# Attention and a GELU layer on one core: eight weight pieces get buffers of their own and are loaded ahead of the second chunk's operands

## The chip, the core and the metric

One core of a Trainium2 chip. The metric is the device time of one execution in microseconds (us), less is better. The core has the engines TensorE (PE, with its weight loads shown as PEld), VectorE (DVE), ScalarE (ACT), GpSimd (POOL) and SyncE (SP); here SP only issues transfers from HBM, which run on 16 DMA engines shared by all queues.

## The reference

Masked attention with a distance bias over 4 batches, 8 heads, 768 positions, 64 values a head; its result, as 3072 rows of 512, goes through two products with a GELU between them.

```python
scores = scale * np.matmul(q, k.transpose(0, 1, 3, 2))
is_global = pos[None, :] < int(n_global)            # n_global = 8
is_local = (rel >= 0) & (rel < int(n_local))        # n_local = 96
...
scores = np.where(is_global | is_local, scores + bias, -1000000000.0)
a = softmax(scores)                                 # written out in the reference
x = (a @ v).transpose(0, 2, 1, 3).reshape(3072, 512)
h = x @ w_in                                        # w_in 512 x 2048, int64-backed words
g = 0.5 * h * (1.0 + erf(h * inv_sqrt2))
return g @ w_out                                    # w_out 2048 x 512
```

## The kernel before

The 3072 rows are done in 12 chunks of 256 rows, three to a batch. The hidden width of 2048 is cut into 8 slices of 256. A step `t` of the list `STEPS` is one chunk with one slice: `m1` makes `h` (24 matmuls for each half, L463), `gelu` turns it into `gh` and `gl` (L473, L474, L174), `m2` adds it to the chunk's sum `acc` (L493). The first two chunks run their slices in turns: (0,0), three empty steps, (1,0), (0,1), (1,1), (0,2) and so on. From the third chunk on, a chunk does its eight slices in a row, while the next chunk's attention is worked off between the steps.

The attention of a chunk c, head pair p, goes through `scores_pair` (PE, L340, tile `s`; then the masked reduction on DVE, L351), `exps` (ACT, L372; the scaling by 1/sum, L381, on DVE for the first two chunks, on POOL after that), `flip` (PE transposes, L391, tile `t`; copied by ACT to `pt`, L395) and `av_pair` (PE, L421). `split` scales the queries on POOL (L168). Chunk 0's operands are loaded by `load_first` into the pool `es`; those of a later chunk by `load` (`qr`, and `kr` in eight transfers for a middle chunk) and `load_v` (`vr`, six transfers), all on SP by L276. The buffers for `kr`, `qr` and `vr` of the later chunks exist once.

The weights arrive as 64-bit words, a slice in four pieces of 512 KB (pieces 0 and 1 are `win`, 2 and 3 `wout`). `load_words` (L176) issues a piece's load on SP (L179). `split_weights` makes a float of the words with one ACT instruction (L204) and three DVE instructions (L210, L212, L214); `part_weights` makes a high and a low half of it (ACT L224, DVE L174). The table `DECODE` says in which step each piece is split. A piece's ACT work is also ordered by hand behind the exponentials and GELUs of earlier steps, and its DVE work behind their reductions:

```python
ins = nc.scalar.activation(out=lw, in_=lw.bitcast(U32), func=AF.Copy, scale=2.0 ** -29).ins
if len(self.his) > 1:
    self.after(ins, self.his[-2], "a piece begins when ScalarE is through with the last but one")
if self.last_table is not None:
    self.after(ins, self.last_table, "a piece comes behind the exponentials of earlier steps")
```

All pieces of slices 0 to 6 go through the four buffers of the pool `ws`, in order. So piece n+4 can be loaded once piece n went through L214. Loads of weights keep their own order on SP, and those of chunk 2 stand behind the last piece of slice 2:

```python
if c == 2:
    self.after(ins.ins, self.word_ins[2, 3], "behind the first slices")
```

The order of instructions on each engine is otherwise made by the scheduler, which walks through the program with estimated times; an engine then works strictly in that order. `warm` matmuls (L359) with no use for the result stand between the first chunks' products, in counts fixed by hand. At the split of slice `LATE` the pool `es` is closed, and weights from that slice on are written where it was.

Of the kernel before, what the change touches and what calls it, by code (L numbers as in the profile page):

```python
# [31 lines left out]
NST = 8  # L32
# [16 lines left out]
DECODE.update({(1, i): i - 1 for i in range(4)})  # L49
DECODE.update({(s, i): 2 * s - 2 + i // 2 for s in range(2, NST) for i in range(4)})  # L50
FILL = {(0, 0, 0): 8, (0, 0, 1): 5, (0, 1, 1): 9, (0, 2, 1): 4, (0, 3, 1): 4, (1, 0, 1): 4}
LATE = 6
NEGMASK = -1000000000.0


# [8 lines left out]
def load_words2(nc, pool, src, name):  # L64
    w = pool.tile([P, 2, 2], I32, name=name + "_w")
    nc.scalar.dma_start(w.rearrange("p i t -> p (i t)"), src.bitcast(I32).partition_broadcast(P))
    return w
# [16 lines left out]
class Fast:  # L84
    def __init__(self, tc, ctx, qT, kT, v, w, out, limits):
        self.tc, self.nc = tc, tc.nc
        self.qT, self.kT, self.v, self.w, self.out = qT, kT, v, w, out
        self.limits = limits
        pool = lambda name, bufs=1, **k: ctx.enter_context(tc.tile_pool(name=name, bufs=bufs, **k))
        self.ctx = ctx  # L90
        self.early = ExitStack()
        self.es = self.early.enter_context(tc.tile_pool(name="es", bufs=1, side="right"))
        self.const = pool("const")
        self.wts = pool("wts")
        self.stg = pool("stg", 3)
        self.nat = pool("nat")
        self.pp = pool("pp", 6)
        self.ptp = pool("ptp", 2)
        self.xp = pool("xp", 3)
        self.gp = pool("gp", 2)  # L100
        self.sm = pool("sm", 2)
        self.words = ExitStack()
        self.ws = self.words.enter_context(tc.tile_pool(name="ws", bufs=4))
        self.ps_acc = pool("ps_acc", 2, space=PSUM)
        self.ps = pool("ps", 6, space=PSUM)
        self.win, self.wout = {}, {}
        self.kt, self.qt, self.vr, self.raw = {}, {}, {}, {}
        self.pt_n, self.pt_t, self.x = {}, {}, {}
        self.stat, self.g, self.h, self.acc = {}, {}, {}, {}
        self.last_table = self.last_word = self.last_dve = self.last_load = None  # L110
        self.his, self.word_ins, self.last_av, self.words_of = [], {}, None, {}
# [62 lines left out]
        return self.nc.vector.tensor_tensor(out=out, in0=in_, in1=hi.bitcast(F32), op=ALU.subtract)  # L174

    def load_words(self, s, i, use):  # L176
        pool, tag = (self.ws, "ws") if use == "w" and s < NST - 1 else (self.stg, "stage")
        w = pool.tile([P, 512, 2], I32, name=f"{use}{s}_{i}", tag=tag)
        ins = self.nc.sync.dma_start(w.rearrange("p f t -> p (f t)"), self.w[s * 4 + i]).ins  # L179
        if use == "w":  # L180
            if self.last_word is not None:
                self.after(ins, self.last_word, "weights in order")
            self.last_word = self.word_ins[s, i] = ins
        elif self.last_load is not None:
            self.after(ins, self.last_load, "behind the loads of earlier steps")
        return w
# [4 lines left out]
    def split_weights(self, s, i):  # L191
        nc = self.nc
        if i == 0:
            if s == LATE:
                self.early.close()
# [324 lines left out]
    def run(self, flag_i):  # L520
        wz = self.wz = self.es.tile([P, 512], F32R, name="wz")
        self.nc.vector.memset(wz.bitcast(F32), 0.0)
        self.warm_ps = self.ps_acc.tile([P, 512], F32, name="warm_ps", tag="ps_acc")
        self.warm(12)
        self.limit_words = load_words2(self.nc, self.const, self.limits, "nn")
        self.load_first()
        self.consts()
        for i in range(4):
            self.load_weights(0, i)
        self.load(1)  # L530
        self.load_v(1)
        for s in range(1, NST - 1):
            for i in range(4):
                self.load_weights(s, i)
        last = len(STEPS)
        for self.T in range(START[0] - 1, last):
            T = self.T
            first = 0 <= T + 1 < last and STEPS[T + 1] is not None
            second = T >= 0 and STEPS[T] is not None
            for (s, i), t in DECODE.items():  # L540
                if T == t + 1:
                    self.part_weights(s, i)
            for (s, i), t in DECODE.items():
                if T == t:
                    if s == NST - 1:
                        self.load_weights(s, i)
                    self.split_weights(s, i)
            if T == last - 8:
                self.flag(flag_i)
            k = T - 16 - GAP  # L550
            if 0 <= k < 64 and k % 2 == 0:
                self.check_load(k // 2)
            if 2 <= k < 66 and k % 2 == 0:
                self.check_words((k - 2) // 2)
            self.att(T, "load")
            self.att(T, "loadv")
            if first:
                self.m1(T + 1, 0)
            self.att(T, "pt", 0)
            if first:  # L560
                self.m1(T + 1, 1)
                self.gelu(T + 1)
            self.att(T, "pt", 1)
            self.att(T, "av")
            self.att(T, "s")
            if second:
                self.m2(T, 0)
            self.att(T, "exp")
            self.att(T, "split")
            if second:  # L570
                self.m2(T, 1)
# [200 lines left out]
```

## Time and profile before

| | us |
|---|---|
| median of 3 runs (698.00, 698.64, 701.43) | 698.64 |
| the profiled execution | 701.12 |
| its span from first to last instruction | 699.4 |
| PE busy in the span | 681.4 |

The profiled execution is a run of its own; 1.7 us of its time lie outside the span. PE is busy for 97% of the span, but its time per matmul is modelled with overlaps, so 97% busy doesn't mean 97% of what it could do. What the profile calls idle is time in which an engine waited for something.

### The profile page before, as it was taken

Reading aid. Unit: us, or ns where it says so; the run is one execution under the profiler, and the core shown is the slowest. Engines: PE = TensorE matmul, PEld = TensorE weight load, DVE = VectorE, ACT = ScalarE, POOL = GpSimd, SP = SyncE. Lnnn points to the kernel's source line nnn. Section 1 sums busy time; section 2 is a strip of 40 time slices with the busy share of each in tenths; the row PEclk is TensorE's granted clock in tenths of the full one; section 3 lists DMA queues with packets and bytes.
Section 4 is the critical chain, followed back from the end, with each engine's and each line's share of the span. In section 5 each row is a group of like instructions: output and inputs, shape, how many; then the busy total and the mean of one; then the engine's idle time right before and its main releaser. Section 6 shows DMA issues by size and latency. Waiting matters only on the chain.

```text
span 699.4 us, 14049 instructions
## 1 busy us (share of the span) xinstructions
PE 681.4 (97%) x5519; PEld 596.6 (85%) x5519; DVE 279.9 (40%) x969; ACT 356.4 (51%) x850; POOL 103.1 (15%) x232
## 2 busy tenths in 40 slices
PE   8989979999999999999999999999999999999996
PEld 6668867888899898898899899898988989988895
DVE  5988897522423423323323324224133243131210
ACT  3886787645435526626536446445356365362211
POOL 3102032201201201211021031031021031010000
PEclk9999999999999999999999999999999999999998
DMA  9728762331504314304144054033053152000000
GB/s 280 210 91 264 254 188 90 103 106 61 136 31 144 99 61 151 100 37 137 50 110 152 17 143 150 3 136 107 30 159 94 58 160 61 31 1 2 32 0 35
DMA packets 66041, 71.25 MB, mean 102 GB/s; under 512 B 32688, under 2 KB 49072, under 8 KB 65968
## 3 DMA queue, kind: packets, MB, share of 16 engines
q1 hardware_dynamic: 61520, 62.80, 29.8%
q10 hardware_dynamic: 4448, 7.48, 3.0%
q8 instruction: 46, 0.75, 0.4%
q14 instruction: 27, 0.22, 0.1%
HBM read 63.97 MB, written 6.29 MB: 100 GB/s over the span
## 4 chain that ended last, share of the span: by engine, by line
PE 89%; ACT 5%; DVE 3%; DMA 2%; issue 1%; POOL 0%; ACTq 0%; POOLq 0%
PE h L463 37%; PE acc L493 36%; PE av L421 6%; PE s L340 5%; PE t L391 4%; ACT n L372 2%; DMA w<-w 2%; PE warm_ps L359 1%; ACT L372 1%; ACT w L204 1%; DVE wb L212 1%; POOL n L381 0%; DVE wb L214 0%; DVE n L351 0%; ACT gh L473 0%
## 5 line engine op out<-in xcount | busy, mean ns | idle before, releaser
L463 PE MATMUL h<-xh,winh 128*128 128x256 f32 x768 | 221.5, 288 | 0.0
L463 PE MATMUL h<-xl,winh 128*128 128x256 f32 x768 | 217.9, 284 | 0.0
L463 PE MATMUL h<-xh,winl 128*128 128x256 f32 x768 | 217.8, 284 | 0.0
L174 DVE TENSOR_TENSOR gl<-gr,gh 128x512 fp32r<-128x512 f32 x96 | 69.0, 719 | 338.8 <-ACT gr L474 338.7
L493 PE MATMUL acc<-wouth,gh 128*128 128x512 f32 x384 | 157.0, 409 | 3.0 <-ACT gh L473 3.0
L463 PEld LDWEIGHTS h<-xh,winh 128*128 128x128 f32 x768 | 147.3, 192 | 5.4 <-issue 0.6
L493 PE MATMUL acc<-woutl,gh 128*128 128x512 f32 x384 | 150.6, 392 | 0.0
L463 PEld LDWEIGHTS h<-xl,winh 128*128 128x128 f32 x768 | 147.4, 192 | 3.7
L493 PE MATMUL acc<-wouth,gl 128*128 128x512 f32 x384 | 149.5, 394 | 0.0
L463 PEld LDWEIGHTS h<-xh,winl 128*128 128x128 f32 x768 | 147.2, 192 | 0.3 <-issue 0.2
L473 ACT ACTIVATE gh<-h 128x512 fp32r<-128x512 f32 x96 | 57.4, 598 | 173.0 <-PE h L463 170.1
L381 POOL TENSOR_SCALAR n<-n,su 128x192 f32<-128x192 f32 (+1 forms) x160 | 73.1, 475 | 457.0 <-ACT n L372 248.6
L395 ACT COPY pt<-t 128x384 f32<-128x384 f32 x96 | 45.6, 482 | 105.2 <-PE t L391 105.2
L493 PEld LDWEIGHTS acc<-wouth,gh 128*128 128x128 f32 x384 | 72.3, 188 | 22.4 <-issue 5.7
L493 PEld LDWEIGHTS acc<-wouth,gl 128*128 128x128 f32 x384 | 72.0, 188 | 16.9 <-issue 0.7
L493 PEld LDWEIGHTS acc<-woutl,gh 128*128 128x128 f32 x384 | 72.4, 189 | 12.5 <-issue 0.2
L372 ACT ACTIVATE n<-n,mn 128x192 f32<-128x192 f32 (+1 forms) x144 | 62.3, 434 | 1.5 <-DVE mn L351 1.3
L351 DVE CUSTOM_DVE_ANT_0 n<-s,pen 128x192 f32<-128x192 f32 (+1 forms) x192 | 55.2, 341 | 8.2 <-PE s L340 8.2
L474 ACT ACTIVATE gr<-h 128x512 f32<-128x512 f32 x96 | 56.9, 593 | 0.0
L391 PE MATMUL t<-ident,n 128*128 128x128 f32 x288 | 48.2, 275 | 4.5 <-POOL n L381 3.0
L421 PE MATMUL av<-pt,vr 64*64 64x64 f32 (+1 forms) x1024 | 46.7, 246 | 2.7 <-ACT pt L395 2.7
L421 PEld LDWEIGHTS av<-pt,vr 64*64 64x64 f32 (+1 forms) x1024 | 35.6, 135 | 13.9 <-issue 6.4
(74 smaller groups left out, 538.9 us busy)
## 6 DMA issues: line engine op xcount, KB each, us to landing
w<-w SPq DMA_DIRECT2D x32, 512.0 KB, 4.6
c<-w SPq DMA_DIRECT2D x32, 512.0 KB, 5.3
out<-o ACTq DMA_DIRECT2D x24, 256.0 KB, 2.0
qr<-qT SPq DMA_DIRECT2D x11, 512.0 KB, 4.0
vr<-v SPq DMA_DIRECT2D x22, 256.0 KB, 4.3
kr<-kT SPq DMA_DIRECT2D x16, 320.0 KB, 5.1
vr<-v SPq DMA_DIRECT2D x19, 192.0 KB, 2.8
kr<-kT SPq DMA_DIRECT2D x36, 64.0 KB, 4.1
```

What stands on the lines that cost most here:

```text
L174: return self.nc.vector.tensor_tensor(out=out, in0=in_, in1=hi.bitcast(F32), op=ALU.subtract)
L340: ins = nc.tensor.matmul(out, lhsT=lhs, rhs=rhs, start=True, stop=True).ins
L351: ins = nc.vector.tensor_tensor_reduce(out=nn[:, j * NK:j * NK + n], in0=sp[hh][:, j, 0:n], in1=pen, scale=-slope(2 * p + hh), scalar=3e38 ...
L372: self.table(nc.scalar.activation(out=nn, in_=nn, func=AF.Exp, bias=mn[:, i:i + 1], scale=-1.0, accum_out=su[:, i:i + 1]))
L381: ins = eng.tensor_scalar(out=nn, in0=nn, scalar1=su[:, i:i + 1], scalar2=0.0, op0=ALU.mult, op1=ALU.add)
L391: nc.tensor.transpose(tp[:, i, :], nn[:, o:o + P], self.ident)
L395: nc.scalar.copy(pt, tp)
L421: ins = nc.tensor.matmul(out, lhsT=lhs, rhs=rhs, start=start, stop=stop, skip_group_check=True).ins
L463: nc.tensor.matmul(hp[:, f, :], lhsT=w[:, d, f * P:(f + 1) * P], rhs=x[:, d, :], start=n == 0, stop=n == 3 * NP - 1)
L473: self.table(nc.scalar.activation(out=gh, in_=hp, func=AF.Gelu))
L474: self.table(nc.scalar.activation(out=gr, in_=hp, func=AF.Gelu))
L493: nc.tensor.matmul(acc, lhsT=g[:, f, ks], rhs=w[:, f, :], start=s == 0 and n == 0, stop=s == NST - 1 and n == 5)
```

## The change

Slices 0 and 1 get eight buffers of their own, one for each piece, in a new pool `rw` that is closed together with `es`. Their eight loads are issued directly behind those of the first chunk, ahead of `load(1)` and `load_v(1)`; before, only slice 0's four were. The four `ws` buffers serve slices 2 to 6 alone. `LATE` goes from 6 to 4, so that slices 4 to 6 are written into the room of `es` and `rw` and slices 0 to 3 stay in `wts`. No computation is added or taken away.

```diff
-LATE = 6
+LATE = 4
+SOON = 2
...
         self.es = self.early.enter_context(tc.tile_pool(name="es", bufs=1, side="right"))
+        self.rw = self.early.enter_context(tc.tile_pool(name="rw", bufs=1, side="right"))
...
-        pool, tag = (self.ws, "ws") if use == "w" and s < NST - 1 else (self.stg, "stage")
+        if use == "w" and s < SOON:
+            pool, tag = self.rw, f"rw{s}_{i}"
+        else:
+            pool, tag = (self.ws, "ws") if use == "w" and s < NST - 1 else (self.stg, "stage")
...
-        for i in range(4):
-            self.load_weights(0, i)
+        for s in range(SOON):
+            for i in range(4):
+                self.load_weights(s, i)
         self.load(1)
         self.load_v(1)
-        for s in range(1, NST - 1):
+        for s in range(SOON, NST - 1):
             for i in range(4):
                 self.load_weights(s, i)
```

## Rows read from the trace of the kernel before

**Rows 1.** The page: busy us of each engine with its share of the span and its number of instructions.

```profile
PE 681.4 (97%) x5519; PEld 596.6 (85%) x5519; DVE 279.9 (40%) x969; ACT 356.4 (51%) x850; POOL 103.1 (15%) x232
```

**Rows 2.** Busy time by stretches: from:to in us, length, then busy us (and instructions) of each engine, the granted TensorE clock as a share of full speed, the share of time that the DMA engines worked, and GB/s.

```profile
10.00:20.00 10.00, 9.27 (x73) 6.25 (x73) 6.83 (x37) 7.26 (x29) 1.85 (x4) 1.00 1.09 350
...
30.00:40.00 10.00, 10.00 (x94) 7.75 (x91) 9.78 (x37) 8.10 (x18) 0.00 (x0) 0.85 0.37 129
40.00:50.00 10.00, 7.90 (x85) 5.13 (x84) 7.64 (x29) 9.69 (x31) 0.00 (x0) 1.00 0.33 104
...
70.00:80.00 10.00, 10.00 (x74) 8.68 (x73) 9.57 (x18) 6.28 (x11) 0.00 (x0) 1.00 0.95 295
...
110.00:130.00 20.00, 19.15 (x167) 15.09 (x166) 15.71 (x38) 13.90 (x28) 4.18 (x4) 1.00 0.09 27
130.00:690.00 560.00, 559.96 (x4591) 500.89 (x4590) 172.08 (x663) 261.78 (x631) 78.64 (x184) 1.00 0.27 82
```

**Rows 3.** What PE waited for, in us in total, times, longest us: the first two rows from 0 to 60 us, the other two, which are all, from 60 to 130 us.

```profile
PE av L421 <- ACT pt L395: 2.7, 3, 1.3
PE t L391 <- DVE n L381: 1.5, 1, 1.5
...
PE acc L493 <- ACT gh L473: 3.0, 2, 2.3
PE t L391 <- POOL n L381: 3.0, 5, 1.5
```

**Rows 4.** The chain of work that ended last, between 78 and 90 us: start, length, what; and the matmul on PE at its end, from the timeline, with the idle time before it in brackets.

```profile
78.69 4.24 DMA w<-w
...
85.02 1.87 ACT n L372 x8
...
89.35 0.50 PE L493 MATMUL acc<-wouth,gh 128*128 128x512 f32 x1 [2.31 <-ACT gh L473]
```

**Rows 5.** What ACT and DVE waited for from 57 to 100 us: in total, times, longest.

```profile
ACT w L204 <- DMA w<-w: 6.7, 8, 1.4
...
DVE wb L210 <- DMA w<-w: 2.6, 2, 2.4
DVE su L374 <- ACT n L372: 1.3, 1, 1.3
```

**Rows 6.** The timeline of SP from 24 us: start, length, line, transfer, count.

```profile
24.83 28.39 SPq L179 DMA_DIRECT2D w<-w  x8
53.32 0.38 SPq L276 DMA_DIRECT2D qr<-qT  x1
...
68.45 52.85 SPq L179 DMA_DIRECT2D w<-w  x17
```

**Rows 7.** Timelines of DVE, ACT and PE: the first reduction of chunk 2's first and of its second head pair (the row before the second one on ACT is the GELU whose DVE work stands ahead of it), and the transpose on PE that waits for that pair.

```profile
81.93 0.34 DVE L351 CUSTOM_DVE_ANT_0 n<-s,pen 128x192 f32<-128x192 f32 x1
...
97.44 0.60 ACT L474 ACTIVATE gr<-h 128x512 f32<-128x512 f32 x1
...
99.56 0.35 DVE L351 CUSTOM_DVE_ANT_0 n<-s,pen 128x192 f32<-128x192 f32 x1
...
104.04 0.33 PE L391 MATMUL t<-ident,n 128*128 128x128 f32 x1 [1.49 <-POOL n L381]
```

**Rows 8.** The timeline of SP from 5 to 25 us: slice 0's words, then the second chunk's operands.

```profile
5.01 4.06 SPq L179 DMA_DIRECT2D w<-w  x4
9.11 0.43 SPq L276 DMA_DIRECT2D qr<-qT  x1
9.94 9.78 SPq L276 DMA_DIRECT2D kr<-kT  x8
19.77 4.95 SPq L276 DMA_DIRECT2D vr<-v  x6
```

**Rows 9.** Single transfers on SP's queue, size, us from issue to landing: slice 0's last piece (issued at 8.64 us), chunk 1's `qr` (at 9.11), its last `kr` (at 18.95) and its last `vr` (at 24.12).

```profile
w<-w SPq DMA_DIRECT2D x1, 512.0 KB, 7.6
qr<-qT SPq DMA_DIRECT2D x1, 512.0 KB, 8.4
...
kr<-kT SPq DMA_DIRECT2D x1, 64.0 KB, 4.2
...
vr<-v SPq DMA_DIRECT2D x1, 256.0 KB, 4.4
```

**Rows 10.** Timelines of PE, DVE and ACT: chunk 1's first scores, their first reduction, their first exponential, then chunk 0's last `av`, which waited for ACT, and chunk 1's first `av`.

```profile
23.94 0.88 PE L340 MATMUL s<-kr,qr 64*64 64x192 f32 x16
...
25.00 0.36 DVE L351 CUSTOM_DVE_ANT_0 n<-s,pen 128x192 f32<-128x192 f32 x1 [0.21 <-PE s L340]
...
26.19 0.47 ACT L372 ACTIVATE n<-n,nmax 128x192 f32<-128x192 f32 x1
...
29.30 0.53 PE L421 MATMUL av<-pt,vr 128*64 128x128 f32 x2 [1.33 <-ACT pt L395]
...
43.54 0.43 PE L421 MATMUL av<-pt,vr 128*64 128x128 f32 x2
```

**Rows 11.** All that ACT waited for from 24 to 50 us: in total, times, longest.

```profile
ACT n L372 <- DVE nmax L351: 1.3, 2, 1.0
ACT gh L473 <- PE h L463: 0.7, 1, 0.7
ACT wouth L224 <- DVE wb L214: 0.6, 1, 0.6
```

## Prediction

> **What bounds the kernel now.** I read the busy shares first: PE holds 681.4 of 699.4 us [rows 1]. Then the same by stretches [rows 2]: from 130 to 690 us PE is busy for 559.96 of 560 us at full clock. Nothing in the change touches that stretch, so every microsecond won or lost has to come from the first 130 us, and whatever is won there reaches the end undiminished. There PE does stop. The reader should see four kinds of waits [rows 3]: before 60 us for the copies of the attention (2.7 us) and for the scaled exponentials of chunk 1 (1.5); after 60 us for a GELU (3.0 us, of it one wait of 2.3) and for chunk 2's scaled exponentials (3.0). Third came the chain that ended last: ahead of the 2.31 us gap at 89.35 it runs back through ACT, through chunk 2's first exponentials, to a DMA of weight words that was under way from 78.69 to 82.93 [rows 4]. Fourth, the waits of ACT and DVE: in 57 to 100 us ACT stands 6.7 us, in eight places, and DVE 2.6 us in front of words that have not landed [rows 5]. So the words are late there, and they bound two engines that PE then waits for.
>
> Why they are late is in SP's timeline [rows 6]. Eight weight loads take from 24.83 to 53.2 us, since each must wait for a buffer; chunk 2's operands stand behind them by order and begin at 53.32; the next words stand behind those, up to 68.45. The DMA engines are only a third busy from 30 to 50 us and 95% busy from 70 to 80 [rows 2]: the transfers come in one heap.
>
> **Slice 1 leaves the ring of four.** No instruction is added; 32 loads of words remain 32. In 24 to 50 us, where slice 1 is split, ACT's waits name no DMA at all [rows 11]. So slice 1's own words were not late, and bringing them earlier is worth 0 in itself: their split is ordered behind the exponentials. The worth lies in what moves up behind them. Slice 2's four loads find their buffers free as soon as SP reaches them, at about 32 us (24.8 and the 5 to 6 us of the next part) where SP was still at them at 53 before. Chunk 2's operands, ordered behind them, need only chunk 1's buffers back, so the heap of 53 to 76 us is pulled apart into the quiet stretch. Slice 3's words are then no longer queued behind that heap; I take ACT's 6.7 us and DVE's 2.6 us of waits on words as gone.
>
> What that does for PE, gap by gap:
> - The 2.31 us at 89.35 [rows 4]. The floor of chunk 2's first exponentials is their reduction, which starts on DVE at 81.93 [rows 7], so they could begin at about 82.3 instead of 85.02 with the table already loaded. That is 2.7 us, more than the gap. It goes: 2.31.
> - The waits on POOL's scaling. The transpose at 104.04 follows the reduction at 99.56 by 4.48 us [rows 7]. DVE is full in front of it. Without the waits of rows 5 it would be 2.6 + 1.3 = 3.9 us further (the 1.3 is its wait for the exponentials just moved), that is 95.66. But the DVE work directly ahead needs the GELU that ends at 97.44 + 0.60 = 98.04; it moves up by the 2.31 only, to 95.73, and takes 0.6: the reduction starts at 96.33, the transpose can start at 100.81. PE gets there at 104.04 - 1.49 - 2.31 = 100.24. A wait of 0.57 is left. The waits around 104 sum to 2.1 (3.0 less the 0.85 idle of 110 to 130 us [rows 2, 3]), so 1.5 is won.
> - The 0.85 us of 110 to 130 us I leave as it is: DVE's lead is used up by then.
>
> Sum: 2.31 + 1.5 = 3.8 us won. Bounds: nothing, if the order on ACT and DVE puts other waits there; 2.31 + 2.1 + 0.85 = 5.3 if every gap goes. I take 3.8, since the DMA row is the direct cause of the larger gap.
>
> **Slice 1's words go ahead of chunk 1's operands.** Four pieces of 0.524 MB are now in front of 15 transfers on the same queue [rows 8]. From 10 to 20 us the DMA engines have no room, share 1.09 at 350 GB/s [rows 2]. Price of 2.10 MB: slice 0's last piece lands at 8.64 + 7.6 = 16.2 and the 512 KB behind it at 9.11 + 8.4 = 17.5 [rows 9], so 1.25 us a piece, 5.0 us for four; by the stretch's rate 2.10/350 = 6.0 us. Chunk 1's last `kr` landed at 18.95 + 4.2 = 23.15 and its first scores ran at 23.94 [rows 9, 10]; so there is 0.8 us to spare and not 5. The scores move to 28.2 to 29.2. `vr` lands at 28.5, then at 33.5 to 34.5, and its first reader is at 43.54 [rows 9, 10]: hidden.
>
> The Trainium skill, "DMA: Bandwidth & Descriptors", section "Queues, rings and completion order", says the same against the change: each DMA engine consumes a queue's descriptors in ring order, so operands can't overtake words. Its figure of some 358 GB/s per core from HBM would make it, as an estimate, 5.9 us; the measured 350 agrees, and the sum by it would be 0.4 us worse.
>
> What the lateness costs. The reduction of chunk 1's first pair starts 1.06 us after the scores and ACT could follow 0.36 us later; the exponentials at 26.19 become 29.6 to 30.6, later by 3.4 to 4.4. ACT had 1.0 + 0.7 + 0.6 = 2.3 us of idle time ahead of the first GELU [rows 11], and chunk 0's last `pt`, which now stood 1.33 us in PE's way [rows 10], can run in the hole instead. If the order fills the hole, 1.1 to 2.1 us are left; I take 1.6. Bounds: a gain of 1.3, if that PE gap goes and nothing replaces it; the whole 5.2 us, if PE stands in front of the scores with the rest behind it.
>
> **`LATE`, pools, addresses.** Slice 4 is written into the room of `es` and `rw`, whose last reader is the split of slice 1. That was done by 53.2 us, when the last load before chunk 2's took slice 1's last buffer; slice 4 is among the last 17 loads, from 68.45 on [rows 6]. The cover is 15 us, so this costs 0; without it ACT would wait for what is missing.
>
> **Sum.** 3.8 won, 1.6 lost: 2.2 us less. Against the profiled execution 701.12 - 2.2 = 698.9; that execution was 2.5 us above the median, and against the median it is 698.64 - 2.2 = 696.4 us. Half a percent, 3.5 us, is about what a measurement of this kernel can tell from no change, so the forecast is a small gain inside that. Chance 0.40; its own range, by 1.1 to 2.1 lost and 2.3 to 5.3 won, is 694.4 to 698.4.
>
> **Rivals.**
> 1. *The hole is filled entirely.* The scheduler knows of the later landing and runs chunk 0's tail first. For: PE idles 2.1 us from 40 to 50 and ACT waits for DVE and PE, so there is slack. Against: ACT is busy 9.69 of 10 us there [rows 2]. Then 0 is lost and 3.8 to 5.3 are won: 693.3 to 694.8, and 690.5 at best with the 1.3 us gap and the low-clock stretch (below) gone too. Chance 0.27.
> 2. *PE parks on chunk 1's scores (the slower side).* In place: 23.94 us. The scores keep their place in PE's order, and chunk 0's transposes, `av` and first `h` wait behind them. For: ACT's order already placed word work where it then waited eight times [rows 5], so the plan takes transfers to be earlier than they are. Price 4.2 to 5.2 us, and then the clock: after PE's gap of 1.33 us the granted clock fell to a mean of 0.85 in 30 to 40 us, the lower of its two levels, 1.2 GHz, for part of it [rows 2, 10], a loss of 1.5 us of work; a longer stop would add another such stretch. (The Trainium skill, "TensorE: Matmul & The Clock Gate", section "HAM oscillation", has the rule that waits for a DMA between groups of matmuls send the clock down; the row agrees.) With 3.8 won later that is 698.64 + 5.2 + 1.5 - 3.8 = 701.5; with only the first gap's 2.3 won it is 703.0. It decides from a stop of 3.8 us on. Chance 0.20, two thirds of it above 700 and about half above 702.1.
> 3. *The words are not the limit.* DVE is 9.57 of 10 us busy from 70 to 80, so earlier words only queue up in front of it, and the gaps move to another wait on DVE. Against: 2.6 us of DVE's own waits were for words. Then 0 is won: 698.64 + 1.6 = 700.2, or 698.6 if the head is hidden. Chance 0.13.
>
> **How the numbers follow.** Time 696.4, the likeliest case. Faster by over 0.5% (below 695.1): rival 1 and a quarter of the forecast's own spread (0.40 x 0.2 = 0.08), 0.35. Slower (above 702.1): half of rival 2 and the worst of rival 3, where both fall together, with an order that loses elsewhere, 0.15. Same: 0.50. Of the low cases those under 691.5 need three gains at once; of the high ones those over 701.5 need the full stop and little won back. Range 691.5 to 701.5.
>
> **What would show it.** Right: SP issues slice 1 at about 9 to 13 us, slice 2 by about 32, chunk 2's operands before 50; ACT's waits on words after 57 us fall from 6.7 to under 2; the gap before `acc` at about 87 is gone; chunk 1's last `kr` lands at 28 or later and its scores run then. Wrong: a PE wait of 3 us or more before chunk 1's scores or directly behind them, or a second low-clock stretch ahead of 30 us (rival 2); ACT and DVE free of word waits while PE still waits 2 us for the GELU (rival 3). The whole forecast falls if the order of chunk 1's exponentials and the first GELU on ACT comes out differently, since that moves all of 26 to 60 us by a table load or more.

## The result: half a percent slower

Over five executions each, the changed kernel took 703.91 us (703.11 to 704.36) and the kernel before 700.46 us (698.00 to 701.43). The ratio is 1.0055, 95% interval 1.0035 to 1.0076: slower, where 2.2 us less was forecast. The profiled execution of the changed kernel took 703.31 us, with a span of 701.5 us. One thing has to be known to read all that follows: over the whole study the kernel before ran 98 times beside the others, with a median of 699.77 us and single executions from 696.5 to 702.4. The 698.64 us against which the sum was made lay 1.1 us too low, and the profiled execution of before, 701.12 us, 1.4 us above that median.

In the profile after, line numbers are five higher from the loads on (scores L345, products `h` L468, GELU L478 and L479, `acc` L498, the split's ACT instruction L209). SP's timeline, start, length, line, transfer, count, answers to [rows 6, 8]:

```profile
5.41 7.32 SPq L184 DMA_DIRECT2D w<-w  x8
13.71 0.38 SPq L281 DMA_DIRECT2D qr<-qT  x1
14.76 11.76 SPq L281 DMA_DIRECT2D kr<-kT  x8
26.57 3.41 SPq L281 DMA_DIRECT2D vr<-v  x6
30.02 2.04 SPq L184 DMA_DIRECT2D w<-w  x4
45.29 0.38 SPq L281 DMA_DIRECT2D qr<-qT  x1
```

The transfers did what the change says. Slice 2 is on its way at 32 us instead of 53, chunk 2's operands start at 45 instead of 53. Chunk 1's last `kr` is issued at 26.02 us and takes 2.6 us: it lands at 28.6, where 28 or later was forecast. The queries, ahead of the keys on the same queue, are later too: POOL starts to scale them, as they land, at 24.68 us instead of 17.62. The first row is POOL's, the second that of the weight load of chunk 1's first scores:

```profile
24.68 2.27 POOL L170 TENSOR_SCALAR qr<-qr,qsc 128x256 f32<-128x256 f32 x4 [15.33 <-DMA qr<-qT]
...
27.75 0.46 PEld L345 LDWEIGHTS s<-kr,qr 64*64 64x64 f32 x8 [1.21 <-POOL qr L170]
```

The scaling was done at 26.95 us (19.47 before). So the first eight scores, at 27.75 us, did not wait for the last keys; the rows name the scaled queries here and DVE in the row of the matmul below. Where this text says late keys, it means the queries and keys of `load(1)` together. The wait of ACT for words between 57 and 100 us fell too, from 6.7 us [rows 5] to 1.9, and DVE no longer waits for words at all. ACT's line (these waits come back below: with the operands in front, where the keys are on time, 4.3 us of them are left):

```profile
ACT w L209 <- DMA w<-w: 1.9, 2, 1.3
```

The time was lost earlier. The windows of after (from:to, length, busy us and instructions of PE, PEld, DVE, ACT, POOL, granted TensorE clock, DMA share, GB/s):

```profile
20.00:30.00 10.00, 8.08 (x70) 4.82 (x70) 8.56 (x30) 6.38 (x21) 2.27 (x4) 0.90 0.94 258
30.00:40.00 10.00, 9.05 (x82) 6.00 (x81) 7.55 (x35) 7.23 (x24) 0.00 (x0) 0.93 0.81 273
40.00:50.00 10.00, 9.63 (x100) 6.76 (x98) 7.64 (x30) 9.90 (x26) 0.49 (x1) 1.00 0.36 102
50.00:60.00 10.00, 7.49 (x40) 6.37 (x40) 8.59 (x21) 5.89 (x13) 2.86 (x4) 0.66 0.34 71
60.00:70.00 10.00, 6.33 (x65) 5.49 (x63) 7.70 (x15) 4.84 (x9) 0.00 (x0) 0.83 0.76 209
...
130.00:690.00 560.00, 559.96 (x4595) 500.40 (x4595) 171.82 (x665) 262.75 (x633) 79.40 (x184) 1.00 0.27 82
```

And windows of before that the rows ahead of the prediction leave out:

```profile
20.00:30.00 10.00, 8.67 (x84) 5.60 (x86) 9.69 (x40) 8.62 (x29) 0.00 (x0) 0.98 0.78 213
50.00:60.00 10.00, 9.77 (x94) 8.55 (x90) 9.07 (x19) 6.13 (x12) 0.01 (x1) 0.83 0.68 230
60.00:70.00 10.00, 9.54 (x59) 8.62 (x60) 7.62 (x12) 5.68 (x11) 5.19 (x4) 1.00 0.87 236
```

From 50 to 70 us PE is busy for 13.8 of 20 us after and 19.3 before. The clock column says the rest: a mean of 0.66 means that PE stood at the lower of its two levels (1.2 of 2.4 GHz) for two thirds of that stretch. What is missing from 1.00 between 20 and 70 us adds up to 6.8 us of full clock after (0.10 + 0.07 + 0.34 + 0.17, times 10) and to 3.4 us before (0.02 + 0.17, and the 0.15 of [rows 2]). The profile of before is not a typical one in this: a second one, below, shows 1.00 from 20 to 80 us. From 130 us on the two are alike to the hundredth.

The places where it begins are PE's waits. Its first rows are the timeline at chunk 1's first scores, the last three those with idle time from 52 to 66 us:

```profile
27.78 1.04 PE L345 MATMUL s<-kr,qr 64*64 64x192 f32 x8 [1.10 <-DVE n L386]
28.75 0.69 PE L396 MATMUL t<-ident,n 128*128 128x128 f32 x2
29.37 0.91 PE L345 MATMUL s<-kr,qr 64*64 64x192 f32 x4
30.21 0.69 PE L396 MATMUL t<-ident,n 128*128 128x128 f32 x2
30.82 0.78 PE L345 MATMUL s<-kr,qr 64*64 64x192 f32 x4
...
52.52 1.08 PE L396 MATMUL t<-ident,n 128*128 128x128 f32 x4 [2.89 <-DVE n L386]
...
64.01 0.39 PE L468 MATMUL h<-xh,winh 128*128 128x256 f32 x1 [1.81 <-ACT xh L454]
65.59 0.58 PE L468 MATMUL h<-xl,winh 128*128 128x256 f32 x1 [1.20 <-DVE xl L176]
```

The sixteen score matmuls that took 0.88 us in one go [rows 10] now stretch from 27.78 to 31.6 us, in three parts with transposes of chunk 0 between them, at the low clock. ACT stands in front of these transposes for 3.4 us, and chunk 1's first exponential, which needs the last part of the scores, starts at 32.14 us instead of 26.19:

```profile
30.77 0.48 ACT L400 COPY pt<-t 128x384 f32<-128x384 f32 x1 [3.40 <-PE t L396]
```

The delay then grows on its way, as ACT's timeline shows for the first, second, seventh and sixteenth GELU. Before:

```profile
37.97 0.60 ACT L473 ACTIVATE gh<-h 128x512 fp32r<-128x512 f32 x1 [0.71 <-PE h L463]
...
59.81 0.60 ACT L473 ACTIVATE gh<-h 128x512 fp32r<-128x512 f32 x1
...
88.70 0.60 ACT L473 ACTIVATE gh<-h 128x512 fp32r<-128x512 f32 x1
...
152.69 0.60 ACT L473 ACTIVATE gh<-h 128x512 fp32r<-128x512 f32 x1 [4.57 <-PE h L463]
```

After:

```profile
41.95 0.60 ACT L478 ACTIVATE gh<-h 128x512 fp32r<-128x512 f32 x1
...
69.38 0.60 ACT L478 ACTIVATE gh<-h 128x512 fp32r<-128x512 f32 x1 [0.95 <-PE h L468]
...
96.11 0.60 ACT L478 ACTIVATE gh<-h 128x512 fp32r<-128x512 f32 x1
...
155.11 0.60 ACT L478 ACTIVATE gh<-h 128x512 fp32r<-128x512 f32 x1 [4.57 <-PE h L468]
```

Late by 4.0 us, then 9.6, 7.4, and 2.4 at the end of it. So some 9.6 us are lost up to 70 us, and 7.2 come back by 155. The greater part of these, 4.8 us, is idle time that a PE which arrives late no longer has: from 80 to 130 us it is idle for 0.45 us after (windows with 10.00, 10.00, 9.62 and 19.93 us busy) and for 5.3 before. Where the rest comes back was not traced. The net, 2.4 us, is what two profiles show, of which that of before was one of its longer executions.

### The profile page after: what moved, and what is told of

Read it like the earlier page. It is cut to its first block, busy times and chain, and to the rows that moved or that the text cites. A ratio compares the mean times of both kernels' runs of the same rounds, so it can differ in the third digit from the quotient of the medians.

```text
span 701.5 us, 14032 instructions
## 1 busy us (share of the span) xinstructions
PE 682.7 (97%) x5519; PEld 596.6 (85%) x5519; DVE 280.0 (40%) x969; ACT 355.9 (51%) x850; POOL 103.6 (15%) x232
## 4 chain that ended last, share of the span: by engine, by line
PE 91%; DVE 4%; ACT 3%; issue 1%; POOL 0%; ACTq 0%
PE h L468 37%; PE acc L498 37%; PE av L426 6%; PE s L345 5%; PE t L396 4%; PE warm_ps L364 2%; ACT n L377 1%; DVE n L356 1%; DVE wb L217 1%; DVE n L386 1%; DVE winl L176 0%; DVE wb L219 0%; ACT L478 0%; DVE wb L215 0%; ACT wouth L229 0%
## 5 line engine op out<-in xcount | busy, mean ns | idle before, releaser
L468 PE MATMUL h<-xh,winh 128*128 128x256 f32 x768 | 221.0, 288 | 2.2 <-ACT xh L454 1.8
L468 PE MATMUL h<-xl,winh 128*128 128x256 f32 x768 | 217.9, 284 | 1.7 <-DVE xl L176 1.7
L468 PE MATMUL h<-xh,winl 128*128 128x256 f32 x768 | 217.4, 283 | 0.0
L176 DVE TENSOR_TENSOR gl<-gr,gh 128x512 fp32r<-128x512 f32 x96 | 67.5, 703 | 342.9 <-ACT gr L479 342.5
L498 PE MATMUL acc<-wouth,gh 128*128 128x512 f32 x384 | 157.2, 409 | 0.7 <-ACT gh L478 0.7
L468 PEld LDWEIGHTS h<-xh,winh 128*128 128x128 f32 x768 | 147.1, 192 | 7.4 <-ACT xh L454 1.9
L468 PEld LDWEIGHTS h<-xl,winh 128*128 128x128 f32 x768 | 147.3, 192 | 6.0 <-DVE xl L176 2.1
L498 PE MATMUL acc<-woutl,gh 128*128 128x512 f32 x384 | 151.1, 394 | 0.0
L498 PE MATMUL acc<-wouth,gl 128*128 128x512 f32 x384 | 150.4, 394 | 0.0
L468 PEld LDWEIGHTS h<-xh,winl 128*128 128x128 f32 x768 | 147.0, 191 | 0.4 <-issue 0.2
L478 ACT ACTIVATE gh<-h 128x512 fp32r<-128x512 f32 x96 | 57.3, 597 | 174.8 <-PE h L468 174.8
L498 PEld LDWEIGHTS acc<-wouth,gh 128*128 128x128 f32 x384 | 72.3, 188 | 20.0 <-issue 5.6
L498 PEld LDWEIGHTS acc<-wouth,gl 128*128 128x128 f32 x384 | 72.2, 188 | 16.6 <-issue 0.3
L498 PEld LDWEIGHTS acc<-woutl,gh 128*128 128x128 f32 x384 | 72.4, 189 | 12.3
L479 ACT ACTIVATE gr<-h 128x512 f32<-128x512 f32 x96 | 56.9, 593 | 0.0
L396 PE MATMUL t<-ident,n 128*128 128x128 f32 x288 | 49.8, 280 | 3.3 <-DVE n L386 2.9
```

The source lines that it names most:

```text
L396: nc.tensor.transpose(tp[:, i, :], nn[:, o:o + P], self.ident)
L468: nc.tensor.matmul(hp[:, f, :], lhsT=w[:, d, f * P:(f + 1) * P], rhs=x[:, d, :], start=n == 0, stop=n == 3 * NP - 1)
L478: self.table(nc.scalar.activation(out=gh, in_=hp, func=AF.Gelu))
L479: self.table(nc.scalar.activation(out=gr, in_=hp, func=AF.Gelu))
L498: nc.tensor.matmul(acc, lhsT=g[:, f, ks], rhs=w[:, f, :], start=s == 0 and n == 0, stop=s == NST - 1 and n == 5)
```

## The experiments

Two theories stood at the start. **The order of the loads at the head:** slice 1's words hold up chunk 1's keys, the rest follows. **The mid-stage:** the new buffers and `LATE` change addresses and the order on ACT and DVE, and that costs the time whatever the head does. A third came up with the clock column: that the lateness itself is cheap and the low clock in the holes is what is paid. The kernels ran in three lots, each on a chip of its own, beside 29 to 35 executions of the kernel before, and every ratio is against these. Last of each kernel's numbers is its mean granted clock over all its timed executions.

**Operands in front, words second.** All of the change but the place of four loads:

```diff
-        for s in range(SOON):
-            for i in range(4):
-                self.load_weights(s, i)
+        for i in range(4):
+            self.load_weights(0, i)
         self.load(1)
         self.load_v(1)
-        for s in range(SOON, NST - 1):
+        for s in range(1, NST - 1):
```

> Slice 1 keeps its own buffers and LATE stays 4; only the order of the loads is undone, so chunk 1's operands are again ahead of slice 1's words. Theory A (the words ahead of the operands cost 8 to 10 us up to 60 us, and the earlier words after that win 4 to 7): the first scores of chunk 1 are back at about 24 us, the PE wait for the GELU at about 87 us is gone, 4 to 7 us less than before. Theory B (PE only seemed to catch up after 70 us because it came late and found everything ready; the words win nothing): within 2 us of before. Theory C (the pools and LATE cost the time, not the order): as slow as the changed kernel, 3 to 4 us above before.

Measured: 700.68 us (697.65 to 703.78, 12 executions), ratio 1.0016 [0.9994, 1.0038], clock 0.9936. The loss is gone; nothing is gained over before either, although the first words come early: in SP's timeline slices 1 and 2 are out by 30.4 us and chunk 2's operands begin at 41.79. Its profiled execution had a span of 695.9 us. What PE waited for from 60 to 130 us, and ACT for words from 57 to 100 us, was this:

```profile
PE t L396 <- POOL n L386: 2.9, 5, 0.8
PE acc L498 <- ACT gh L478: 0.7, 1, 0.7
...
ACT w L209 <- DMA w<-w: 4.3, 4, 2.3
```

The GELU gap of [rows 3, 4] is gone, POOL's waits stay at 2.9 us. The waits on words did not go: 4.3 us of ACT's 6.7 are left, and 0.8 of DVE's 2.6. So the 1.9 us of the changed kernel was its lateness, and not words that had come in time.

**Keys in front, words before the values.**

```diff
-        for s in range(SOON):
-            for i in range(4):
-                self.load_weights(s, i)
+        for i in range(4):
+            self.load_weights(0, i)
         self.load(1)
+        for i in range(4):
+            self.load_weights(1, i)
         self.load_v(1)
```

> As the changed kernel, but slice 1's words stand between chunk 1's keys and queries and its values. Theory A: the keys land at 23 us as before, the values at some 33 us with their first reader at 43 us, so it is as fast as the run with all operands first, 4 to 7 us below before. If lateness of the values matters too, it lies between that run and the changed kernel.

Measured: 700.37 us, ratio 1.0008 [0.9988, 1.0027], clock 0.9938. The values may be late for nothing, as the prediction had it: it is `load(1)`, the queries and keys.

**Half of slice 1 ahead.** Pieces (1,0) and (1,1) ahead of the operands, the other two behind them.

```diff
-        for s in range(SOON):
-            for i in range(4):
-                self.load_weights(s, i)
+        for n in range(6):
+            self.load_weights(n // 4, n % 4)
         self.load(1)
         self.load_v(1)
+        for n in range(6, 8):
+            self.load_weights(n // 4, n % 4)
```

> As the changed kernel, but only two of slice 1's four pieces are ahead of chunk 1's operands, two behind. Theory A with a cost in proportion: the keys land 2.5 us late instead of 5, half of the loss, 0 to 2 us below before. If the loss is a matter of the order that the schedule falls into, and not of the microseconds, it need not lie between the two: either all of the loss or none.

Measured: 701.06 us, ratio 1.0016 [0.9997, 1.0036], clock 0.9956. The last key lands 3.3 us later than in before by its trace (issued at 23.26 us, 3.2 to landing; 2.5 was expected). With 0.8 us to spare, that cost less than can be told from nothing. Chunk 1's first scores stand together on PE, as in [rows 10], and wait for the keys once:

```profile
24.87 1.08 PE L345 MATMUL s<-kr,qr 64*64 64x192 f32 x12 [0.68 <-DVE xl L176]
26.53 0.54 PE L345 MATMUL s<-kr,qr 64*64 64x192 f32 x4 [0.57 <-DMA kr<-kT]
```

**Three pieces ahead.** The same with 7 in place of 6, in another lot.

> Three of slice 1's four pieces ahead of chunk 1's operands, one behind. Keys land about 3.7 us later than in before (three pieces at 1.25 us). Theory, that the loss starts only when PE's holes get long enough for the clock to fall: either near two pieces ahead (701) or near four (703.6), with extra low-clock stretches in the first 70 us in the second case and none in the first. Rival, that each piece costs its share of lateness: 701.0 plus a half of 2.6, about 702.3, with no more low clock than with two pieces.

Measured: 703.17 us (700.49 to 704.73), ratio 1.0035 [1.0017, 1.0053], clock 0.9874. Its windows:

```profile
20.00:30.00 10.00, 7.38 (x68) 4.66 (x68) 7.30 (x27) 5.77 (x18) 2.42 (x4) 0.82 0.90 242
30.00:40.00 10.00, 9.34 (x80) 6.64 (x77) 7.74 (x34) 7.03 (x24) 0.00 (x0) 0.84 0.87 304
...
50.00:60.00 10.00, 7.70 (x78) 6.43 (x74) 9.38 (x24) 6.95 (x18) 3.31 (x4) 0.83 0.42 89
60.00:70.00 10.00, 6.70 (x64) 5.67 (x62) 7.87 (x16) 4.66 (x8) 0.00 (x0) 0.70 0.74 193
70.00:80.00 10.00, 9.80 (x46) 8.68 (x47) 9.34 (x18) 7.74 (x16) 0.00 (x0) 0.79 0.58 206
```

With three pieces the low clock is there in the same stretches as with four, and from 70 to 80 us besides; this profile, of 704.05 us, is one of the slower executions. The executions fall into two groups, six at 700.5 to 702.5 us and six at 703.9 to 704.7, the first with clocks of 0.986 to 0.993, the second of 0.983 to 0.987. The mean clock over all executions is 0.9956 at two pieces, 0.9874 at three and 0.9848 at four (the run of the unchanged after below). So the step in the clock lies between two and three pieces, which speaks for the theory. It does not show it, for two reasons. By time, the ratio at three pieces lies midway between those at two and at four (1.0055 in the first lot, 1.0071 below), as a loss in proportion to the pieces would have it. And the scheduler's order changes at the same place: with three pieces, as with four, matmuls of chunk 0 stand between chunk 1's first scores, and PE later has a stop of 1.8 us for `xh` that no profile with two pieces or with the operands in front shows. That all or none of the loss comes with the order is the rival that the expectation for two pieces had named. No run moves the keys and holds the order, so it stays open whether the step is one of the holes or of the order.

**`LATE` alone.** The kernel before with `LATE = 4`; the order of instructions on PE, ACT and DVE is that of before.

> The kernel before with LATE 4 instead of 6 and nothing else. Theories A and B: no difference, within 1 us. Theory C: slower by 3 us.

Measured: 698.61 us, ratio 0.9985 [0.9966, 1.0004], clock 0.9947. Costs nothing, as predicted. In its profile the GELU gap was missing as well, with the words only 2 us earlier (the last group of loads in [rows 6] starts at 66.47 us instead of 68.45):

```profile
PE t L391 <- POOL n L381: 2.7, 5, 1.2
PE acc L493 <- ACT gh L473: 0.7, 1, 0.7
```

**Both kernels again, unchanged.**

> The kernel before, unchanged, for a second trace of the same program. If the 2.31 us wait of PE for the GELU at 89 us and ACT's 6.7 us of waits on words belong to the kernel, they stand here as well, and the times agree with before within 0.5 us. If they belong to that one execution (701.12 us, above the median), the wait is under 1 us here, as in the run with LATE alone, whose engines have the same order of work.

> The changed kernel, unchanged, on the chip of the other runs. 3 to 4.5 us above before, with chunk 1's first scores at 27.5 us or later and three or more low-clock stretches of the matmul engine between 25 and 70 us, if these belong to the kernel and not to one execution.

Measured: before again 700.63 us (12 executions), ratio 1.0025 [1.0008, 1.0042] against 29 executions of the very same program in the same lot; after again 703.52 us (703.08 to 704.53, 6), ratio 1.0071 [1.0056, 1.0086], clock 0.985. The first says what a ratio here is worth: 0.25% between identical programs, more than its own interval admits. The loss of after stands clear of that in both lots, at 0.55% and 0.71%. The second profile of after has PE's holes in the same places with other lengths (0.82 and 2.12 us before chunk 1's scores, 3.1 us at the transposes) and the low clock too, 0.91, 0.74 and 0.83 in the windows from 20, 30 and 50 us. The second profile of before has 3.1 us of GELU waits and 1.5 us of POOL's, where the first had 3.0 and 3.0. It also has the stop of 1.33 us of [rows 10], in the same place and as long, and yet the window behind it is at the upper level, where the first had 0.85:

```profile
30.11 0.43 PE L421 MATMUL av<-pt,vr 128*64 128x128 f32 x2 [1.32 <-ACT pt L395]
...
30.00:40.00 10.00, 9.40 (x95) 6.95 (x95) 9.99 (x39) 8.47 (x20) 0.00 (x0) 1.00 0.35 116
```

**Keys earlier than in before.** Slice 0's last two pieces moved behind chunk 1's keys, in the kernel before:

```diff
-        for i in range(4):
+        for i in range(2):
             self.load_weights(0, i)
         self.load(1)
+        for i in range(2, 4):
+            self.load_weights(0, i)
         self.load_v(1)
```

> The kernel before, with chunk 1's queries and keys loaded ahead of slice 0's last two pieces; the order of work on PE, ACT and DVE is the same. The keys land 2.5 us earlier, at about 20.6 us, the two pieces at some 22 to 23 us with a first reader at 25. If the keys are on the path of the kernel before, 1 to 2.5 us less; if they had 0.8 us to spare and only lateness beyond that costs, no difference over 0.7 us, and faster is not to be had at this place.

Measured: 698.59 us, ratio 1.0002 [0.9988, 1.0016]; the first scores ran at 23.90 us, 0.04 earlier than in [rows 10]. With 0.8 us to spare the keys were not what the scores waited for, so only lateness counts.

**The clock held in two holes.** The changed kernel with 16 more `warm` matmuls, whose result nobody reads: 5 ahead of chunk 1's first scores, 11 behind the transposes of head (1,5).

```diff
+HOLD = {(1, 5): 11}
...
+        if (c, p) == (1, 0):
+            prev = self.warm(5, self.last_av)
...
+        if (c, h) in HOLD:
+            if c == 1:
+                self.warm_ps = self.bank([P, 512], "hold_ps")
+            self.warm(HOLD[c, h], ins)
```

> The changed kernel with 16 more warm matmuls whose result nothing reads: five between chunk 0's last but one product with the values and chunk 1's first scores, eleven behind the transposes of chunk 1's sixth head, that is in the two places where PE stood still before its low-clock stretches. Theory D (most of the 4 us is the clock that falls in these holes): the mean granted clock rises from 0.985 to 0.992 or more and the time falls by 2 to 4 us, to about before. Rival (the lateness itself, in ACT's and DVE's order, costs the time): the clock rises and the time falls by less than 1 us.

Measured: 699.03 us (698.45 to 701.48, 12), mean 699.78, ratio 1.0012 [0.9999, 1.0025], clock 0.9931. In the same lot after again had a mean of 703.64 us: added work made it 3.9 us faster. The order on DVE and ACT shifts a little with the edit, so the kernel before got the same one:

> The kernel before with the same 16 warm matmuls at the same two places (5 ahead of chunk 1's first scores, 11 behind the transposes of chunk 1's head 5). Theory, that they help the changed kernel only by holding the clock in the holes that late keys make: before has no such holes, so no gain, 0 to 2 us slower for 3.4 us of added matmuls (about 0.21 us each at full clock) that stand partly in the way; 699 to 702. Rival, that such matmuls or the shift of the order that comes with them speed any version by some 4 us: 695 to 696.

Measured: 699.78 us, ratio 0.9987 [0.9973, 1.0001], clock 0.9942. The edit wins 0.9 us there by its ratio (1.9 at most by the interval), so of the 3.9 us about 3 (2.0 at least) belong to the holes that only the changed kernel has. The control is not quite the order of before: its profile has the stop for `xh` as well, 1.3 us for `xl` behind it, and a clock of 0.83 from 60 to 70 us, with the queries and keys as early as in before and no loss in time.

```profile
PE h L470 <- ACT xh L456: 1.6, 1, 1.6
```

So this stop comes with the order and not with late keys, and the kernel was no slower for it.

**A third hole.** What was left in the profile of the kernel with two holds was a low clock from 60 to 71 us, behind waits of 1.45 and 1.40 us for `xh` and `xl`:

```profile
60.00:70.00 10.00, 7.81 (x30) 6.93 (x31) 7.80 (x16) 6.05 (x11) 0.00 (x0) 0.55 0.98 284
```

So 12 more went behind chunk 1's last `av`:

```diff
+        if (c, p) == (1, 3):
+            self.warm_ps = self.bank([P, 512], "hold_ps2")
+            self.warm(12, self.last_av)
```

> The changed kernel with the 16 warm matmuls of the held kernel and 12 more behind chunk 1's last av, where the held kernel's PE waited 1.45 and 1.40 us for xh and xl at about 58 to 62 us and the clock then stayed low for about 10 us. Theory, that what is left of the held kernel's loss is that stretch: the low clock of 60 to 71 us is gone, 4 to 5 us of lost work come back less up to 1 us of delay, 695 to 697, below the kernel before. Rival, that PE then merely waits later for the words, the GELU and POOL, because ACT and DVE set the pace up to 100 us: 699 to 700, with the low clock gone and the waits larger by as much.

Measured: 699.74 us (699.38 to 700.06, 12), ratio 0.9998 [0.9983, 1.0014], clock 0.9981. Two of its windows, its PE waits from 60 to 130 us, and its first exponentials of chunk 1 and its sixteenth GELU on ACT:

```profile
50.00:60.00 10.00, 9.82 (x94) 7.89 (x93) 10.00 (x26) 6.87 (x15) 0.88 (x2) 1.00 0.45 109
60.00:70.00 10.00, 8.62 (x64) 8.07 (x64) 9.32 (x19) 7.02 (x12) 0.00 (x0) 1.00 0.69 223
```

```profile
PE acc L508 <- ACT gh L488: 1.4, 1, 1.4
PE t L399 <- POOL n L389: 0.4, 1, 0.4
```

```profile
30.43 0.46 ACT L380 ACTIVATE n<-n,nmax 128x192 f32<-128x192 f32 x1 [0.55 <-DVE nmax L359]
...
151.60 0.60 ACT L488 ACTIVATE gh<-h 128x512 fp32r<-128x512 f32 x1 [4.57 <-PE h L478]
```

The first scores run at 27.54 us, as late as in after (27.78), but the exponentials behind them 1.7 us sooner (30.43 for 32.14). The clock is at its upper level in every window up to 690 us, and yet the mean is that of the kernel with two holds: the 695 to 697 us of the first theory did not come. The stretch from 60 us, which the control had too, was worth nothing. The rival got the time right, though not the way to it, since the waits from 60 us on did not grow (1.8 us, where after had 4.0): the 12 matmuls themselves now fill the place in which PE stood. What is left over is lateness, with the order that goes with it. The profile with operands in front is the one to hold against it, since it shows no low clock in its first 130 us either:

```profile
149.54 0.60 ACT L478 ACTIVATE gh<-h 128x512 fp32r<-128x512 f32 x1 [4.57 <-PE h L468]
```

Its sixteenth GELU is 2.06 us earlier. So with the clock held, late keys (with their order and the 28 added matmuls) cost 2.06 us between these two profiles; without, the same GELU of after comes another 3.51 us later (155.11). Of the 5.6 us between after and operands in front, then, some 3.5 go with the clock, and an unknown part of these with the shifted order. By the means the same kernels say 703.6 for after, 699.7 held, and 700.75 for operands in front; the last one is no lower than the second, and its clock is one part of that (a mean of 0.9936, where its profiled execution had 0.998).

## Why the prediction was wrong

It failed in its sum: 696.4 us, range 691.5 to 701.5, where 703.91 came. The 7.5 us fall on three places: the base, 1.1 us too low; the 3.8 us of the mid-stage that did not come; and the head, where 1.6 us were put in and 4.1 stand (703.91 less the median of 699.77, if nothing was won later; the runs do not separate the two).

**Right, step by step.** All that is lost is lost ahead of 130 us. SP reaches slice 2 at 30 to 32 us and chunk 2's operands at 45. The keys land at 28.6 us and the scores run at 27.8 in the first of three parts (28.2 to 29.2 was forecast for the whole). The values are hidden. `LATE` and the pools cost nothing. The order of chunk 1's exponentials and the first GELU did not cost a table load. One sign came by luck: ACT's waits for words fall to 1.9 us, under the 2 that were named, but only because ACT came later.

**The step "What the lateness costs" failed.** It took 1.6 us, on the grounds that PE's hole would be filled with chunk 0's tail and ACT had 2.3 us of slack. The size was not bad, with 2.06 by the runs that hold the clock, but in part by luck, for the way was another: chunk 0's last transposes, which were to run in the hole, stand behind the first scores, and the first GELU came 4.0 us late instead of 1.1 to 2.1 (2.6 with the clock held: 40.61 us for 37.97). The queries, later by 7.1 us, were not looked at by themselves. What the step put at nothing is the clock. The order did pull one group of `av` ahead of the scores, but not enough to close the hole, and each stop of 1 to 3 us (1.10, 2.89, 1.81, 1.20) stands in or next to a stretch at the lower level: around 30 us, from 50 and from 60, where before had two, around 30 behind a gap of 1.33 us [rows 2, 10] and from 50. Rival 2 named just this mechanism and its sign, and priced it at one more stretch, 1.5 us. It was 3.4 us more than before in the first 70 us of the two profiles; by the mean clocks over all executions, 0.985 against 0.994 to 0.996 for before in the three lots, it is 6 to 8 us of full clock in 700. That is more than the whole loss in time, so a microsecond of clock is not one of time here. Rival 2 was to decide from a stop of 3.8 us on; it decided with waits of 0.82 and 1.10 us in front of the scores, and 0.82 and 2.12 in the second profile. (The Trainium skill, "TensorE: Matmul & The Clock Gate", section "HAM oscillation", has waits between groups of matmuls send the clock down; its case is a wait for a DMA, where the rows of PE's stops name DVE and ACT. The trace agrees in direction, 0.66 in the window in which the stop of 2.89 us ends, where before had 0.83.) That the stops alone decide is not shown: the same stop of 1.3 us in the two profiles of before came once with a low clock behind it and once without.

**The step of the mid-stage failed in three places.** First, in the changed kernel the premise was gone: chunk 2's first exponentials were to begin at 82.3 us instead of 85.02 [rows 4], and began at 90.77, since everything ahead of them was late. The GELU gap vanished, as forecast, but because PE came later. Second, without that lateness the exponentials did begin where it was said (82.06 us with operands in front), the GELU wait fell from 3.0 to 0.7 us, and POOL's waits stayed, 2.9 us against the 1.4 that were to be left. Yet the median is that of before. Third, "I take ACT's 6.7 us and DVE's 2.6 us of waits on words as gone" did not hold there: 4.3 and 0.8 were left. The gap is the open row. Of five profiles in which the words come as in before or nearly so, it stands in three (3.0, 3.1 and 2.5 us) and not in two (0.7 and 0.7), and one of these two, `LATE` alone, has before's order of instructions throughout. Both profiles of before itself have it. Rival 3, that words are not the limit, fits the time, but no run took the words out of the way with the keys in time; whether the early words win a little that an interval of 0.2% can't show, stays open.

**The base.** The sum took waits seen in an execution of 701.12 us away from a median of three that was lower, so that part of the waits may not have been in the executions of that median at all. The times speak for it: in the lot of the operands-first run 15 executions of before had a granted clock of 0.996 or 0.997, six of them at 696.9 to 697.9 us and nine at 699.5 to 700.4, with none between. At the same clock something of some 2.5 us is there in one execution and not in another; the second profile of before, with 0.997, 699.61 us and the gap, would belong to the longer ones. That it is the GELU gap is not shown, since no execution of the shorter ones was profiled.

**What stays open:** why the GELU gap stands in both profiles of before and not in that of `LATE` alone, whether the loss needs the order that comes with late keys, and where the operands-first kernel's longer executions (up to 703.8 us) lose what its profiled one did not. No version beat before by more than two lots of the same program differ.

## What to carry to other kernels

When a change delays work at the head of a kernel, price the delay twice: once as lateness, which later slack can swallow in part (9.6 us at 70 us and 2.4 at 155 here), and once as the holes that it makes in TensorE, behind which the clock can fall (about 3 of the 3.9 us here). To tell the two apart, fill the holes with matmuls that do no work, and put the same fill into the kernel without the holes: if added work makes the one faster and not the other, it points to the clock. And a wait in a profile is not yet a gain: the GELU gap stood in both profiles of before, was gone in three changed versions, and their times stayed within 0.2% of before.

## What the runs showed of the hardware

- Stops of 1.1 to 2.9 us on TensorE went along with granted clocks of 0.66 to 0.93 in windows of 10 us; where the holes were filled, every window up to 130 us showed 1.00.
- A stop alone does not decide. The stop of 1.33 us at 29.3 us in the first profile of before had 0.85 in the next window, the one of 1.32 us in the same place of the second 1.00; operands in front had stops of 1.4 and 1.3 us and 1.00 in every window up to 130 us.
- The place of the low-clock stretches differs between executions of one program: 0.66 and 0.83 in the windows from 50 and 60 us in the first profile of after, 0.83 and 0.83 in the second, and 0.93 against 0.74 from 30 us.
- The kernel whose clock was held in three places had executions within 0.7 us (699.38 to 700.06), beside 5.1 us of the kernel before on the same chip (696.96 to 702.10). That fits a spread that comes in part from the clock, and no more than fits: executions of before with the same clock of 0.996 or 0.997 lie up to 3.5 us apart in the lot of the operands-first run.
- Twelve executions of a program stood 0.25% [0.08%, 0.42%] above 29 others of the same program in one lot.
